# Attention, gating and experts given to the scheduler as one program instead of three stages

## The chip, the cores and the metric

The kernel runs on one core of a Trainium2 chip. The core has five instruction queues that run side by side and meet only at semaphores: TensorE (PE in the profile, its weight loads PEld), VectorE (DVE), ScalarE (ACT), GpSimd (POOL) and SyncE (SP, which here only starts DMAs). The metric is the device time of one execution in microseconds (us). Before the change it is 3069.19 us, the median of four runs that lie between 3068.82 and 3069.36 us.

## The reference: what is computed

Inputs are `q`, `k`, `v` of shape (8, 8, 576, 64) (batch B, heads H, sequence S, head dimension) and random features `omega` (128, 64). Attention is linear: each row of q and k becomes 128 positive features, and softmax is replaced by two small products per head.

```python
h  = x*scale @ omega.T - sum((x*scale)**2)/2
phi = exp(h - max(h)) / sqrt(128)
num = phi(q) @ (phi(k).T @ v)
den = phi(q) @ phi(k).sum(rows)
x   = num / (den + 1e-6)             # heads side by side: (8, 576, 512)
```

The result x goes into a mixture of E = 8 experts. Each token has 8 gate logits and a local gate. Where the local gate is below a half (and at the first token of a sequence) the token takes the expert with the largest logit, otherwise it keeps the expert of the token before it. The output is the softmax weight of that expert times `relu(x @ w1[e]) @ w2[e]`, with w1 of shape (512, 1024) and w2 of shape (1024, 512) for each expert. The kernel computes all 8 experts for every token and adds them up with weights that are zero for all but one.

## The kernel before, in words

The kernel is written in a framework that takes a program, records what reads and writes what, puts the instructions of each engine in an order of its own choice, and adds the semaphores. What limits its choice is the dependences and the tile pools: a tile in a pool of n buffers can be started only when the user of the buffer n tiles ago is done. Copies written as `nc.any` are given to ACT or DVE by the scheduler. Every engine then runs its list strictly in order, and an instruction that waits holds up all that stand behind it on that engine.

The work stands in three blocks, each in a `with` of its own pools, so that a block starts only when the pools of the one before it are given back (lines are those of the kernel before):

- **Attention** (lines 76 to 135). For each of 8 x 8 heads, five tiles of up to 128 rows (four of 128 and one of 64). A *k tile*: transpose k on PE (L87), copy (L89), project with omega (L91), row maximum on DVE (L93), exponential on ACT (L95), and accumulate the product with v into `kv_ps` (L99). A *q tile*: transpose (L108), copy (L110), project (L112), exponential (L119), transpose (L121), copy (L123), product with the head's kv (L125), reciprocal and scaling on DVE (L127, L129), transpose back (L131), copy (L133), and a store into `x_bridge`, a DRAM tensor of shape (512, tokens) (L134). All products of this block are float32. PSUM: five buffers for the tiles named `proj`, three for `kv_ps`.
- **Gating** (lines 138 to 203). For each batch b, five tiles: load x from DRAM, logits on PE (L154), softmax and expert choice in small DVE and ACT steps, two transposes (L181, L184); then a scan along the sequence in ten doubling steps on DVE (L189, L190), one reduction over partitions on POOL (L194). The weights are transposed to token rows (L200).
- **Experts** (lines 206 to 245). All weights lie in SBUF as bfloat16; their loads are issued on POOL at the very start of the kernel. For each of 9 groups `tg` of 512 tokens: load x (L223), and for each expert eight h groups (four matmuls over the 512 inputs into one bank, L231; ReLU on ACT into `hsb`, L234), each followed by four matmuls into four y banks (L236). After the eighth group DVE adds each of the four y banks, weighted, to `acc` (L240). Then `acc` is stored (L244). PSUM: two h banks and four y banks; SBUF: two x buffers and two `acc` buffers.

Of the kernel before, what the change touches and what calls it, by code (L numbers as in the profile page):

```python
# [18 lines left out]
def kernel(  # L19
# [12 lines left out]
    nc = tc.nc  # L32
# [7 lines left out]

# [12 lines left out]
    NTG = (T + TG - 1) // TG  # L53
    assert T % TG == 0

    x_dram = nc.dram_tensor("x_bridge", (D, T), F32, kind="Internal").ap()

# [4 lines left out]
    nc.vector.tensor_copy(ident_bf, ident)  # L62
    omegaT = consts.tile([Dh, M], F32)
# [11 lines left out]

    with tc.tile_pool(name="attn_sb", bufs=6) as sb, \
         tc.tile_pool(name="attn_sb2", bufs=4) as sb2, \
         tc.tile_pool(name="attn_ps", bufs=5, space=bass.MemoryType.PSUM) as ps, \
         tc.tile_pool(name="attn_ps2", bufs=3, space=bass.MemoryType.PSUM) as ps2:
        for b in range(B):  # L80
            for h in range(H):
                kv_ps = ps2.tile([M, Dh + 1], F32)
                for ti, (s0, nt) in enumerate(stile):
                    k_nat = sb.tile([128, Dh], F32, name="qk_nat")
                    nc.sync.dma_start(out=k_nat[:nt], in_=k[b, h, ds(s0, nt), :])
                    kT_ps = ps.tile([128, 128], F32, name="proj")
                    nc.tensor.transpose(kT_ps[:Dh, :nt], k_nat[:nt], ident[:nt, :nt])  # L87
                    kT = sb.tile([Dh, 128], F32, name="qkT")
                    nc.any.tensor_copy(kT[:, :nt], kT_ps[:Dh, :nt])  # L89
                    proj = ps.tile([128, M], F32, name="proj")  # L90
                    nc.tensor.matmul(proj[:nt], lhsT=kT[:, :nt], rhs=omegaTs, start=True, stop=True)  # L91
                    mxn = sb.tile([128, 1], F32, name="mxn")
                    nc.vector.reduce_max(mxn[:nt], proj[:nt], axis=AX, negate=True)  # L93
                    kp = sb.tile([128, M], F32, name="qkp")
                    nc.scalar.activation(kp[:nt], proj[:nt], Act.Exp, bias=mxn[:nt])  # L95
                    v_aug = sb.tile([128, Dh + 1], F32, name="v_aug")
                    nc.sync.dma_start(out=v_aug[:nt, :Dh], in_=v[b, h, ds(s0, nt), :])
                    nc.vector.memset(v_aug[:nt, Dh:Dh + 1], 1.0)
                    nc.tensor.matmul(kv_ps, lhsT=kp[:nt], rhs=v_aug[:nt],  # L99
                                     start=(ti == 0), stop=(ti == NST - 1))  # L100
                kv_sb = sb2.tile([M, Dh + 1], F32)
                nc.any.tensor_copy(kv_sb, kv_ps)

                for ti, (s0, nt) in enumerate(stile):
                    q_nat = sb.tile([128, Dh], F32, name="qk_nat")
                    nc.sync.dma_start(out=q_nat[:nt], in_=q[b, h, ds(s0, nt), :])
                    qT_ps = ps.tile([128, 128], F32, name="proj")
                    nc.tensor.transpose(qT_ps[:Dh, :nt], q_nat[:nt], ident[:nt, :nt])  # L108
                    qT = sb.tile([Dh, 128], F32, name="qkT")
                    nc.any.tensor_copy(qT[:, :nt], qT_ps[:Dh, :nt])  # L110
                    proj = ps.tile([128, M], F32, name="proj")
                    nc.tensor.matmul(proj[:nt], lhsT=qT[:, :nt], rhs=omegaTs, start=True, stop=True)  # L112
                    ksq = sb.tile([128, Dh], F32, name="qksq")
                    sq = sb.tile([128, 1], F32, name="sq")
# [161 lines left out]
```

## Time and profile before

| what | value |
|---|---|
| median of 4 runs | 3069.19 us |
| the profiled execution, its own time | 3069.36 us |
| its span in the trace | 3067.3 us |
| busy PE / PEld / DVE / ACT / POOL | 2372.0 / 1222.0 / 691.6 / 863.9 / 86.8 us |
| instructions | 28764 |
| mean granted TensorE clock | 0.999 |

The profile is one execution. Its page gives busy time of each engine, the span in 40 slices, and the chain of work that ended last. Other views of the same trace list groups of instructions by line (count, busy time, mean of one, idle time before them and who ended it), the single instructions in order of time, and the busy times in chosen stretches. A matmul's duration in the trace runs to the modelled end of its result, so that two matmuls that follow each other overlap; what a matmul costs PE is read from the distance of two starts.

### The profile page before, as it was taken

What the parts mean: (1) busy time and instruction counts of PE and PEld (TensorE: products, weight loads), DVE (VectorE), ACT (ScalarE), POOL (GpSimd) and SP (SyncE); (2) the same over time, 40 slices, a digit from 0 to 9 for tenths busy, and PEclk for the clock granted to TensorE, in tenths of its full rate; (3) what the DMA queues carried; (4) which work ended last, traced back from release to release, by engine and by line L of the source; (5) the groups of instructions that cost most, each with busy time, mean ns of one, the idle gap of its engine ahead of it and who ended that gap; (6) DMA issues with size and microseconds to landing.
All of it is one profiled execution on the core that took longest, in us unless ns stands there. A gap on an engine that the chain in (4) does not pass through costs nothing.

```text
span 3067.3 us, 28764 instructions
## 1 busy us (share of the span) xinstructions
PE 2372.0 (77%) x8792; PEld 1222.0 (40%) x8884; DVE 691.6 (23%) x2980; ACT 863.9 (28%) x2541; POOL 86.8 (3%) x147
## 2 busy tenths in 40 slices
PE   5666666666666666666666666669999999999999
PEld 3443433434434334344343344433333333333333
DVE  1121211211212112122121123751222221221212
ACT  2222222222222222222222222223333333333333
POOL 5100000000000000000000000110000000000000
PEclk9999999999999999999999999999999999999999
DMA  9400100001000001000010001210000000000000
GB/s 176 86 20 21 22 20 21 22 19 22 20 21 22 20 21 22 19 22 21 20 22 20 21 22 44 69 32 1 21 21 1 21 21 1 21 21 2 20 14 14
DMA packets 208298, 80.11 MB, mean 26 GB/s; under 512 B 153872, under 2 KB 199440, under 8 KB 208144
## 3 DMA queue, kind: packets, MB, share of 16 engines
q1 hardware_dynamic: 189136, 56.77, 8.2%
q0 software_dynamic: 19008, 21.50, 4.2%
q8 instruction: 70, 1.15, 0.2%
q14 instruction: 84, 0.69, 0.1%
HBM read 80.79 MB, written 18.87 MB: 32 GB/s over the span
## 4 chain that ended last, share of the span: by engine, by line
PE 74%; ACT 10%; DVE 9%; issue 5%; DMA 1%; SPq 0%; ACTq 0%; POOL 0%; DVEq 0%; POOLq 0%
PE y_ps L236 17%; PE h_ps L231 16%; PE proj L112 8%; PE proj L91 8%; PE proj L125 7%; PE proj L121 5%; PE proj L131 4%; ACT qkp L119 4%; PE kv_ps L99 3%; PE proj L87 3%; DVE oa L129 3%; ACT qpT L123 3%; DVE qkT L110 2%; DVE rden L127 2%; ACT oaT L133 2%
## 5 line engine op out<-in xcount | busy, mean ns | idle before, releaser
L236 PE MATMUL y_ps<-w_all,hsb 128*128 128x512 bf16 x2266 | 545.4, 381 | 3.9 <-ACT hsb L234 1.5
L231 PE MATMUL h_ps<-xT,w_all 128*128 128x512 bf16 x2250 | 541.0, 380 | 6.2 <-DMA xT<-x_bridge 3.5
L234 ACT ACTIVATE hsb<-h_ps 128x512 bf16<-128x512 f32 x576 | 343.8, 597 | 675.7 <-PE h_ps L231 671.6
L240 DVE SCALAR_TENSOR_TENSOR acc<-y_ps,w_all_t,acc 128x512 f32<-128x512 f32 x288 | 196.3, 745 | 771.9 <-PE y_ps L236 754.8
L231 PEld LDWEIGHTS <-w_all 128*128 128x128 bf16 x2304 | 225.6, 98 | 276.3 <-DMA xT<-x_bridge 2.9
L112 PE MATMUL proj<-omegaTs,qkT 64*128 64x128 f32 (+1 forms) x640 | 246.6, 487 | 110.9 <-DVE qkT L110 109.2
L236 PEld LDWEIGHTS <-hsb 128*128 128x128 bf16 x2304 | 179.5, 98 | 339.0 <-ACT hsb L234 199.7
L125 PE MATMUL proj<-kv_sb,qpT 128*128 128x65 f32 (+1 forms) x640 | 206.8, 425 | 110.1 <-ACT qpT L123 110.1
L91 PE MATMUL proj<-omegaTs,qkT 64*128 64x128 f32 (+1 forms) x640 | 247.0, 487 | 51.9 <-ACT qkT L89 48.4
L131 PE MATMUL proj<-ident,oa 128*64 128x128 f32 (+1 forms) x320 | 128.3, 401 | 186.3 <-DVE oa L129 185.1
L121 PE MATMUL proj<-ident,qkp 128*128 128x128 f32 (+1 forms) x320 | 145.6, 455 | 141.5 <-ACT qkp L119 133.0
L127 DVE RECIPROCAL rden<-proj 128x1 f32<-128x1 f32 (+1 forms) x320 | 53.3, 167 | 815.9 <-PE proj L125 815.9
L133 ACT COPY oaT<-proj 64x128 f32<-64x128 f32 (+1 forms) x320 | 79.5, 249 | 550.0 <-PE proj L131 550.0
L112 PEld LDWEIGHTS proj<-omegaTs,qkT 64*128 64x128 f32 (+1 forms) x640 | 145.7, 287 | 221.9 <-DVE qkT L110 208.2
L125 PEld LDWEIGHTS proj<-kv_sb,qpT 128*128 128x128 f32 (+1 forms) x640 | 146.3, 289 | 197.6 <-ACT qpT L123 197.6
L119 ACT ACTIVATE qkp<-proj,sq 128x128 f32<-128x128 f32 (+1 forms) x320 | 117.3, 366 | 350.0 <-PE proj L112 350.0
L91 PEld LDWEIGHTS proj<-omegaTs,qkT 64*128 64x128 f32 (+1 forms) x640 | 146.1, 288 | 121.2 <-ACT qkT L89 113.6
L99 PE MATMUL kv_ps<-v_aug,qkp 128*128 128x65 f32 (+1 forms) x640 | 179.6, 382 | 0.4 <-ACT qkp L95 0.3
L99 PEld LDWEIGHTS kv_ps<-v_aug,qkp 128*128 128x128 f32 (+1 forms) x640 | 172.0, 328 | 18.6 <-issue 17.4
L93 DVE TENSOR_REDUCE mxn<-proj 128x1 f32<-128x128 f32 (+1 forms) x320 | 92.8, 290 | 341.4 <-PE proj L91 341.3
L89 ACT COPY qkT<-proj 64x128 f32<-64x128 f32 (+1 forms) x320 | 79.5, 249 | 275.1 <-PE proj L87 266.0
L121 PEld LDWEIGHTS proj<-ident,qkp 128*128 128x128 f32 (+1 forms) x320 | 58.4, 182 | 235.3 <-ACT qkp L119 235.2
(59 smaller groups left out, 1359.7 us busy)
## 6 DMA issues: line engine op xcount, KB each, us to landing
out_dram<-acc SPq DMA_DIRECT2D x36, 256.0 KB, 4.9
w_all<-in_moe_w_dram POOLq DMA_DIRECT2D x32, 256.0 KB, 7.0
qk_nat<-in_k_dram SPq DMA_DIRECT2D x256, 32.0 KB, 1.7
v_aug<-in_v_dram SPq DMA_DIRECT2D x256, 32.0 KB, 1.9
w_all<-in_moe_w_dram POOLq DMA_DIRECT2D x64, 128.0 KB, 7.8
qk_nat<-in_q_dram SPq DMA_DIRECT2D x256, 32.0 KB, 1.7
x_bridge<-oaT SPq DMA_DIRECT2D x256, 32.0 KB, 1.8
xT<-x_bridge SPq DMA_DIRECT2D x128, 64.0 KB, 2.0
```

Of the source, the lines that this page charges most:

```text
L91: nc.tensor.matmul(proj[:nt], lhsT=kT[:, :nt], rhs=omegaTs, start=True, stop=True)
L99: nc.tensor.matmul(kv_ps, lhsT=kp[:nt], rhs=v_aug[:nt], start=(ti == 0), stop=(ti == NST - 1))
L112: nc.tensor.matmul(proj[:nt], lhsT=qT[:, :nt], rhs=omegaTs, start=True, stop=True)
L119: nc.scalar.activation(qp[:nt], proj[:nt], Act.Exp, bias=sq[:nt])
L121: nc.tensor.transpose(qpT_ps[:, :nt], qp[:nt], ident[:nt, :nt])
L125: nc.tensor.matmul(o_ps[:nt, :Dh + 1], lhsT=qpT[:, :nt], rhs=kv_sb, start=True, stop=True)
L131: nc.tensor.transpose(oaT_ps[:Dh, :nt], oa[:nt], ident[:nt, :nt])
L133: nc.any.tensor_copy(oaT[:, :nt], oaT_ps[:Dh, :nt])
L231: nc.tensor.matmul(h_ps, lhsT=w1_all[:, e, c, ts(fc, 128)], rhs=xT[:, c, :], start=(c == 0), stop=(c == DC - 1))
L234: nc.scalar.activation(hsb, h_ps, Act.Relu)
L236: nc.tensor.matmul(y_ps[st][:128, :], lhsT=hsb[:, ts(st, 128)], rhs=w2_all[:, e, fc, :], start=(fc == 0), stop=(fc == FC - 1))
L240: nc.vector.scalar_tensor_tensor(acc[:, st, :], in0=y_ps[st], scalar=w_all_t[:, tt, e:e + 1], in1=acc[:, st, :], op0=Alu.mult, op1=Alu.add)
```

## The change

Three things change, and the arithmetic of the attention and gating steps stays the same.

1. All pools are opened once, at the top, and stay open to the end. The eight PSUM banks are divided among the three parts for the whole time: four for attention (`tp`, each tile now a full bank), one for `kv`, one for gating (`lg`), one for h (`h_ps`), one for y (`y_ps`). SBUF buffers: 4 instead of 6 in attention, one x buffer and one `acc` for the experts instead of two. The parts become functions `attn(b)`, `gating(b)` and `moe(tg)`; the program text calls attention and gating batch by batch, then the nine expert groups. Nothing but dependences and buffers now keeps the scheduler from putting expert work among later attention work.
2. In the experts, `hsb` holds all eight h groups of an expert (two buffers), and the four y banks are filled one after another from one bank, eight matmuls each.
3. In batch 0 only, each of the seven float32 PSUM tiles of a k and q tile pair first gets a matmul of the identity with a block of zeros (`fill`), 128x512 bfloat16. It writes zeros that the real matmul then overwrites.

In the changed kernel the attention lines are L110 (transpose k), L116 (project k), L124 (kv), L134, L140, L151, L157, L165 (the five PE steps of a q tile), the fills L109, L115, L133, L139, L150, L156, L164; gating has L181, L205, L208, L225 on PE; the experts have L242 (h), L244 (ReLU), L248 (y), L251 (weighted add), L234 (load x), L236 (clear `acc`), L254 (store).

```diff
-    with tc.tile_pool(name="attn_sb", bufs=6) as sb, \
-         tc.tile_pool(name="attn_sb2", bufs=4) as sb2, \
-         tc.tile_pool(name="attn_ps", bufs=5, space=bass.MemoryType.PSUM) as ps, \
-         tc.tile_pool(name="attn_ps2", bufs=3, space=bass.MemoryType.PSUM) as ps2:
...
+    fill = consts.tile([128, 512], BF)
+    nc.vector.memset(fill, 0.0)
...
+    a_sb = ctx.enter_context(tc.tile_pool(name="a_sb", bufs=4))
+    a_sb2 = ctx.enter_context(tc.tile_pool(name="a_sb2", bufs=3))
+    a_ps = ctx.enter_context(tc.tile_pool(name="a_ps", bufs=4, space=bass.MemoryType.PSUM))
+    a_ps2 = ctx.enter_context(tc.tile_pool(name="a_ps2", bufs=1, space=bass.MemoryType.PSUM))
+    g_sb = ctx.enter_context(tc.tile_pool(name="g_sb", bufs=2))
+    g_pb = ctx.enter_context(tc.tile_pool(name="g_pb", bufs=1))
+    g_ps = ctx.enter_context(tc.tile_pool(name="g_ps", bufs=1, space=bass.MemoryType.PSUM))
+    m_x = ctx.enter_context(tc.tile_pool(name="m_x", bufs=1))
+    m_h = ctx.enter_context(tc.tile_pool(name="m_h", bufs=2))
+    m_o = ctx.enter_context(tc.tile_pool(name="m_o", bufs=1))
+    m_psy = ctx.enter_context(tc.tile_pool(name="m_psy", bufs=1, space=bass.MemoryType.PSUM))
+    m_psh = ctx.enter_context(tc.tile_pool(name="m_psh", bufs=1, space=bass.MemoryType.PSUM))
...
+                kT_ps = a_ps.tile([128, 512], F32, name="tp")
+                if b == 0:
+                    nc.tensor.matmul(kT_ps, lhsT=ident_bf, rhs=fill, start=True, stop=True)
+                nc.tensor.transpose(kT_ps[:Dh, :nt], k_nat[:nt], ident[:nt, :nt])
...
+    def moe(tg):
+        t0 = tg * TG
+        xT = m_x.tile([128, DC, TG], BF, name="mxT")
...
+        for e in range(E):
+            hsb = m_h.tile([128, FC, TG], BF, name="hsb")
+            for fc in range(FC):
+                h_ps = m_psh.tile([128, TG], F32, name="h_ps")
+                for c in range(DC):
+                    nc.tensor.matmul(h_ps, lhsT=w1_all[:, e, c, ts(fc, 128)],
+                                     rhs=xT[:, c, :], start=(c == 0), stop=(c == DC - 1))
+                nc.scalar.activation(hsb[:, fc, :], h_ps, Act.Relu)
+            for st in range(ST):
+                y_ps = m_psy.tile([128, D], F32, name="y_ps")
                 for fc in range(FC):
...
+                    nc.tensor.matmul(y_ps, lhsT=hsb[:, fc, ts(st, 128)],
+                                     rhs=w2_all[:, e, fc, :], start=(fc == 0), stop=(fc == FC - 1))
+                tt = tg * ST + st
+                nc.vector.scalar_tensor_tensor(acc[:, st, :], in0=y_ps, scalar=w_all_t[:, tt, e:e + 1],
+                                               in1=acc[:, st, :], op0=Alu.mult, op1=Alu.add)
...
+    for b in range(B):
+        attn(b)
+        gating(b)
...
+    for tg in range(NTG):
+        moe(tg)
```

Three places show how the instructions move. The names are the tiles; what stands in brackets is the semaphore that an instruction waits for.

The first is PE in the middle of the attention. Before, a 128-row q tile is five matmuls in a row, from one transpose of q to the next:

```order
L108 MATMUL proj<-ident,qk_nat 64x128 [waits DMAHW4_49]
L112 MATMUL proj<-omegaTs,qkT 128x128 [waits DVE_49]
L121 MATMUL proj<-ident,qkp 128x128 [waits Activation_49]
L125 MATMUL proj<-kv_sb,qpT 128x65 [waits Activation_49]
L131 MATMUL proj<-ident,oa 64x128 [waits DVE_49]
```

Now the same five steps have expert matmuls between them. In the tile shown, which belongs to the 27th of the 64 heads, there are 1, 3, 2 and 3 of them in the four gaps ("..." stands for the rest of a gap):

```order
L134 MATMUL tp<-ident,qk_nat 64x128 [waits DMAHW2_49]
L242 LDWEIGHTS w_all
L242 MATMUL h_ps<-mxT,w_all 128x512
L140 MATMUL tp<-omegaTs,qkT 128x128 [waits Activation_49]
L248 LDWEIGHTS hsb
L248 MATMUL y_ps<-w_all,hsb 128x512 [waits DVE_49]
...
L151 MATMUL tp<-ident,qkp 128x128 [waits Activation_49]
...
L157 MATMUL tp<-kv_sb,qpT 128x65 [waits Activation_49]
...
L165 MATMUL tp<-ident,oa 64x128 [waits DVE_49]
```

What moved: of the 4608 expert matmuls, 3250 stand ahead of the last attention matmul in PE's list (the first of them in batch 0's fifth head), and 1358 behind it. On average a gap of a 128-row q tile holds 2.2, 2.6, 1.7 and 3.2 of them, and the gap between L110 and L116 of a k tile holds 2.0.

The second place is PE in batch 0, where there is no expert work yet. The fills stand in the gaps, and the transpose and projection of the next q tile (L134, L140) now stand ahead of the transpose back of this one (L165):

```order
L157 MATMUL tp<-kv_sb,qpT 128x65 [waits Activation_49]
L134 MATMUL tp<-ident,qk_nat 64x128 [waits DMAHW5_49]
L139 LDWEIGHTS ident_bf
L139 MATMUL tp<-fill,ident_bf 128x512 [waits PE_49]
L140 MATMUL tp<-omegaTs,qkT 128x128 [waits Activation_49]
L165 MATMUL tp<-ident,oa 64x128 [waits DVE_49]
...
L151 MATMUL tp<-ident,qkp 128x128 [waits Activation_49]
```

What moved: in batch 0 a q tile no longer ends before the next one begins. In batches 1 to 7 the old order stands (L165, then L134). The fills are 280 in all.

The third is PE in the experts when the attention is over. Before, two h groups of four and two y groups of four alternate, and h has two banks (the numbers 18651 and 18662 are two tiles in two buffers):

```order
L231 MATMUL h_ps_18651<-xT_18574,w1_all_16124 128x512
...
L231 MATMUL h_ps_18662<-xT_18574,w1_all_16124 128x512
...
L236 MATMUL y_ps_18581<-w2_all_16125,hsb_18656 128x512
L236 MATMUL y_ps_18582<-w2_all_16125,hsb_18656 128x512
L236 MATMUL y_ps_18583<-w2_all_16125,hsb_18656 128x512
L236 MATMUL y_ps_18584<-w2_all_16125,hsb_18656 128x512
L236 MATMUL y_ps_18581<-w2_all_16125,hsb_18667 128x512
```

Now each h group waits for ACT and each y group for DVE, since the bank is the same one:

```order
L242 MATMUL h_ps_21949<-mxT_21573,w1_all_86 128x512 [waits Activation_49]
...
L248 MATMUL y_ps_21926<-w2_all_87,hsb_21847 128x512 [waits DVE_49]
...
L242 MATMUL h_ps_21955<-mxT_21573,w1_all_86 128x512 [waits Activation_49]
...
L248 MATMUL y_ps_21985<-w2_all_87,hsb_21936 128x512 [waits DVE_49]
...
L242 MATMUL h_ps_21961<-mxT_21573,w1_all_86 128x512 [waits Activation_49]
L242 MATMUL h_ps_21961<-mxT_21573,w1_all_86 128x512
...
L248 MATMUL y_ps_21985<-w2_all_87,hsb_21936 128x512
L242 MATMUL h_ps_21967<-mxT_21573,w1_all_86 128x512 [waits Activation_49]
```

What moved: for one expert the list is now h4 y8 h4 y8 h4 y8 h4 y3 h4 y1 h4 y1 h4 y1 h4 y1 y1 (a letter with the number of matmuls). Eight h groups each reuse one bank, four y groups each reuse one bank, and four of the h groups have only a single y matmul behind them.

291 lines of the change are left out of this document (136 added, 155 removed).

## Prediction

> **What bounds the kernel now.** I read the page first, for PE's share, its clock and the chain:
>
> ```profile
> PE   5666666666666666666666666669999999999999
> PEclk9999999999999999999999999999999999999999
> PE 74%; ACT 10%; DVE 9%; issue 5%; DMA 1%; SPq 0%; ACTq 0%; POOL 0%; DVEq 0%; POOLq 0%
> ```
>
> There are two regimes: PE busy at six tenths for two thirds of the span, then full. The clock is full in every slice. The busy times in three stretches give the stages (columns: stretch and length, then busy time and count of PE, PEld, DVE, ACT, POOL, then clock, DMA share, GB/s):
>
> ```profile
> 13.00:1880.00 1867.00, 1265.96 (x3832) 740.75 (x3832) 369.71 (x2167) 476.32 (x1724) 46.38 (x88) 1.00 0.15 30
> 1880.00:2043.00 163.00, 95.36 (x444) 76.11 (x444) 111.50 (x509) 42.51 (x240) 18.57 (x14) 1.00 0.25 60
> 2043.00:3067.30 1024.30, 1010.66 (x4516) 405.11 (x4608) 209.69 (x296) 343.82 (x576) 16.48 (x32) 1.00 0.06 14
> ```
>
> 13 us of start, attention to about 1880, gating to 2043, experts to the end. Only the experts fill PE; attention is a chain, as PE's instructions in order of time show (start, duration):
>
> ```profile
> 1009.18 0.42 PE L87 MATMUL proj<-ident,qk_nat 128*64 128x128 f32 x1
> ...
> 1012.22 0.42 PE L87 MATMUL proj<-ident,qk_nat 128*64 128x128 f32 x1
> 1012.43 0.53 PE L99 MATMUL kv_ps<-v_aug,qkp 128*128 128x65 f32 x2
> 1012.99 0.79 PE L91 MATMUL proj<-omegaTs,qkT 64*128 64x128 f32 x2
> 1013.71 0.42 PE L87 MATMUL proj<-ident,qk_nat 128*64 128x128 f32 x1
> ...
> 1016.55 0.42 PE L108 MATMUL proj<-ident,qk_nat 128*64 128x128 f32 x1
> ...
> 1020.89 0.42 PE L108 MATMUL proj<-ident,qk_nat 128*64 128x128 f32 x1
> 1021.75 0.79 PE L112 MATMUL proj<-omegaTs,qkT 64*128 64x128 f32 x2 [0.44 <-DVE qkT L110]
> 1023.06 0.48 PE L121 MATMUL proj<-ident,qkp 128*128 128x128 f32 x1 [0.52 <-ACT qkp L119]
> 1023.89 0.69 PE L125 MATMUL proj<-kv_sb,qpT 128*128 128x65 f32 x2 [0.35 <-ACT qpT L123]
> 1025.16 0.42 PE L131 MATMUL proj<-ident,oa 128*64 128x128 f32 x1 [0.58 <-DVE oa L129]
> 1025.38 0.42 PE L108 MATMUL proj<-ident,qk_nat 128*64 128x128 f32 x1
> ...
> 1038.34 0.42 PE L87 MATMUL proj<-ident,qk_nat 128*64 128x128 f32 x1
> ```
>
> A head takes 1038.34 - 1009.18 = 29.16 us, and 64 x 29.16 = 1866, which is the stage. Its five k tiles take 1016.55 - 1009.18 = 7.37; a 128-row q tile takes 1025.38 - 1020.89 = 4.49. In the q tile each step waits for ACT or DVE to bring back the last one's result. What a step occupies is less than its duration: a transpose lasts 0.42, but the next matmul starts 0.22 later (1025.16 to 1025.38). Taking that tail of 0.2 off, the five steps occupy 0.22 + 0.59 + 0.28 + 0.49 + 0.22 = 1.8 us, and PE is free for 0.64, 0.72, 0.55 and 0.78 us in the four gaps, 2.7 us in all.
>
> **What an expert matmul and its waits cost.** Rows of the expert stage, in order of time:
>
> ```profile
> 2167.13 1.89 PE L231 MATMUL h_ps<-xT,w_all 128*128 128x512 bf16 x8
> 2168.25 0.60 ACT L234 ACTIVATE hsb<-h_ps 128x512 bf16<-128x512 f32 x1 [2.05 <-PE h_ps L231]
> ...
> 2168.91 1.90 PE L236 MATMUL y_ps<-w_all,hsb 128*128 128x512 bf16 x7
> ...
> 2170.64 1.89 PE L231 MATMUL h_ps<-xT,w_all 128*128 128x512 bf16 x8
> ```
>
> Sixteen matmuls take 2170.64 - 2167.13 = 3.51 us, 0.219 each (one record of the y row is missing). 4608 of them are 1009 us, the stage. The first h group of four has entered PE by 2167.13 + 0.88 = 2168.01; its ReLU starts at 2168.25 and y, which reads it, at 2168.91. So **one use of an h bank costs 0.90 us** after the last matmul has entered. For a y bank:
>
> ```profile
> 2059.72 1.90 PE L236 MATMUL y_ps<-w_all,hsb 128*128 128x512 bf16 x8
> ...
> 2061.08 2.73 DVE L240 SCALAR_TENSOR_TENSOR acc<-y_ps,w_all_t,acc 128x512 f32<-128x512 f32 x4 [17.04 <-ACT hsb L234]
> ```
>
> ```profile
> L240 DVE SCALAR_TENSOR_TENSOR acc<-y_ps,w_all_t,acc 128x512 f32<-128x512 f32 x288 | 196.3, 745 | 771.9 <-PE y_ps L236 754.8
> ```
>
> The fifth matmul completes the first bank and has entered by 2059.72 + 5 x 0.219 = 2060.82; DVE starts 0.26 later and takes 0.745. With 0.05 for the semaphore (the gap from the ReLU's end at 2168.85 to y is 0.06) **one use of a y bank costs 1.06 us**. Before, other banks covered both.
>
> **The change part by part.**
>
> *Batch 0 (eight heads, no expert work).* The 280 fills are 280 x 0.219 = 61 us of PE. They stand in gaps: five per q tile are 1.1 us against 2.7 free. They gain nothing, since the clock is 1.00 already. What does gain is the new order, in which the next L134 and L140 go ahead of L165: the period is then L125's 0.49, then 0.86 (transpose to projection), 1.31 and 0.83 (the steps of the rows above), 3.49 us for 4.49. A k tile loses: L124 no longer fills the wait for the copy but stands with two fills ahead of L116: 0.21 + 0.56 + 0.44 + 0.59 = 1.8 us for 1.49. A head: five k tiles 9.0, first q tile 4.3, three at 3.5, the 64-row one 3.0: 26.8. I take **220 us for eight**; bounds 210, and 8 x 29.16 + 61 = 294 if nothing of it overlaps.
>
> *Batches 1 to 7 (56 heads, with 3250 expert matmuls, 58 a head).* The 9.7 expert matmuls of a q tile are 2.1 us against 2.7 free; gap by gap 0.48 of 0.64, 0.57 of 0.72, 0.37 of 0.55, 0.70 of 0.78. The chain therefore stays near 4.49. In a k tile two of them (0.44) hide in the wait between L110 and L116 (1012.22 to 1012.99, 0.77 between starts), but L124 now stands behind L116: 0.77 + 0.59 + 0.56 = 1.92 for 1.49. Five make 9.3 for 7.37. A head is then **31.1 us** if nothing collides. What is added per head:
>
> - ACT and DVE run in order. 7.3 ReLUs of 0.6 and 3.6 weighted adds of 0.745 make 7.1 us a head. They cost nothing where they fall while PE works, all 7.1 if each holds up a step of the chain. Most gaps leave ACT or DVE free for the better part of a microsecond, so I take 1.5, near the lower end. In it are the waits for the one h and y bank: between two uses there is mostly more than one attention step, over 1.06 us.
> - Gating now runs beside attention, and its 163 us as a stage go. Its PE and DVE work does not:
>
> ```profile
> L154 PE MATMUL lg<-wg,xT 128*128 128x9 f32 (+1 forms) x320 | 66.9, 336 | 40.0 <-ACT pe L165 17.0 <-issue 15.5 <-DMA xT<-x_bridge 4.0
> L181 PE MATMUL proj<-ident,sv 128*8 128x128 f32 (+1 forms) x40 | 14.4, 359 | 14.1 <-DVE sv L179 6.0 <-DVE rst L170 2.9 <-ACT seg_a L182 2.7
> L184 PE MATMUL proj<-ident,pe 128*8 128x128 f32 (+1 forms) x40 | 15.0, 375 | 3.6 <-ACT seg_a L182 2.4
> L189 DVE TENSOR_TENSOR seg_b<-seg_a 8x575 f32<-8x575 f32 (+4 forms) x40 | 26.8, 669 | 2.5 <-ACT seg_a L182 2.3
> ```
>
>   The PE rows are 96 us, 12 per batch; the scan's maxima, two such groups, about 6 per batch on DVE. Half of both on the path is 9 per batch, 1.1 a head (bounds 0 and 2.3). The SP queue also carries the loads of x and the stores of the result among the loads of q, k and v, which stand up to four buffers ahead; nothing is added.
> - One x buffer: a group's load starts when the last h of the group before is done.
>
> ```profile
> 2040.16 4.46 POOL L223 DMA_DIRECT2D xT<-x_bridge  x8 [2.15 <-DVE w_all L197]
> ...
> 2043.32 0.61 PE L231 MATMUL h_ps<-xT,w_all 128*128 128x512 bf16 x1 [2.24 <-DMA xT<-x_bridge]
> ...
> 2045.81 2.44 PE L231 MATMUL h_ps<-xT,w_all 128*128 128x512 bf16 x5 [1.02 <-DMA xT<-x_bridge]
> ```
>
>   The last part is there 5.65 us after the issue, and about 2.5 us of y work stands ahead: 3.2 a group, six groups, 0.35 a head. POOL's list has the weight loads first, as before, then x loads and gating's reductions, each of which stands where its input comes late anyway. The single `acc` waits for a store and a clear while eight h groups of the next expert run, and costs nothing unless DVE stands at the clear.
>
> The sum is 31.1 + 1.5 + 1.1 + 0.35 = 34.05, and **56 x 34.05 = 1907 us**. Bounds: 31.1 x 56 = 1742, and with 7.1, 2.3 and 0.6 in full 41.1 x 56 = 2302.
>
> *The rest of the experts (1358 matmuls, 21.2 experts).* In the pattern h4 y8 h4 y8 h4 y8 h4 y3 h4 y1 h4 y1 h4 y1 h4 y1 y1 each y group starts 0.88 after the last: short by 1.06 - 0.88 = 0.18, four times. An h group with y8 ahead waits for nothing; three with one y ahead are short by 0.90 - 0.22 = 0.68, and so is the last y1; one with three ahead by 0.06. In all 0.72 + 2.72 + 0.06 = 3.5 us on 64 x 0.219 = 14.0. 21.2 x 17.5 = 371; two x reloads and the last gating add about 12. **383 us**, where the kernel before would take 297.
>
> *End.* Before, the last add and store are
>
> ```profile
> 3061.30 2.73 DVE L240 SCALAR_TENSOR_TENSOR acc<-y_ps,w_all_t,acc 128x512 f32<-128x512 f32 x4 [11.33 <-PE y_ps L236]
> 3062.07 2.31 SPq L244 DMA_DIRECT2D out_dram<-acc  x4
> ```
>
> so the span ends 3.3 us after the last add; with 1.0 for the add, 4 to 5 us.
>
> Sum: 13 + 220 + 1907 + 383 + 5 = 2528 of span. The profiled execution's own time is 2.1 us above its span and 0.2 us from the median, so the time is **2530 us**, 17.6% below before. Put otherwise: 712 us of expert work and 163 of gating go under the attention, which grows by about 275 for it; the tail gives back 86.
>
> [...] The attention stretch has a gap of 0.35 to 0.58 us before four of five matmuls and still shows clock 1.00. [...]
>
> **The rivals.**
>
> - *ACT and DVE collide.* For it: 7.1 us a head of long instructions in in-order queues that also carry every chain step. Against it: ACT is busy 476 of 1867 us in attention. With two thirds of them on the path (4.8 for 1.5), the head is 37.3 and the time 2715; with all and the upper bounds 41.1 and 2925.
> - *Single banks in an in-order queue (slower).* If each h group and each y group in PE's list stands there until its bank is free, with the attention matmul behind it: 7.3 x 0.90 + 3.6 x 1.06 = 10.4 a head. With the 3.0 above, 31.1 + 10.4 + 3.0 = 44.5, 2492 for 56, and 3115 us. It is slower from (3067 - 621) / 56 = 43.7 a head on. Against it: mostly an attention step, which waits anyway, stands between two uses.
> - *The clock halves* in the tail: 64 x 0.219 more per expert, 21.2 x 14 = 297, 2825 us. The rows at 1.00 are against it.
> - *Less is lost*: collisions and gating wholly hidden, 31.1 to 32 a head, 2365 to 2415 us.
> - *The interleaving is not there*, because something holds the expert work back: then only the 163 of gating could go, and the tail's losses (72 x 3.5 = 252) make it slower; but PE's list fixes the order, and PE cannot leave it.
>
> **How the numbers follow.** Forecast, 32.3 to 38 a head, 2430 to 2750: 0.81. Collisions above that: 0.08. Less lost: 0.05. Slower: 0.04. Halved clock: 0.02. The range is 2430 to 2750. About 0.2% can be told from no change in this kernel; faster by more 0.95, within 0.01, slower 0.04.
>
> **What would show it.** Right: no separate gating stage; attention of batches 1 to 7 from about 235 to 2140 us, 34 us from one L110 of a head to the next; a q tile of 128 rows at 4.5 to 5; in the tail 17.5 us per expert with 0.6 to 0.7 idle before an L242 group, ended by ACT; clock 1.00. Wrong: idle before L242 or L248 ended by ACT or DVE while attention runs, of many tenths per group; chain steps that wait for a ReLU or an add; PE long idle for a DMA.

## The result, and the profile after

The median after is 2082.91 us, against 3069.18 before: a ratio of 0.6785 (95% interval 0.6775 to 0.6795). The forecast, 2530 in a range from 2430 to 2750, had the sign right and missed the size by 447 us; the time lies below the range. The one execution of the changed kernel that was first profiled was disturbed (4086 us, its bfloat16 matmuls some 0.62 us apart throughout), so the trace read here, called *after*, is of the same kernel run again: 2090.42 us, span 2088.7.

Its page: PE's busy row and its granted clock in 40 slices.

```profile
PE   6899999999999999999999999999999998888887
PEclk9898799999999999999988899999999999999999
```

Where PE was busy for six tenths of two thirds of the span, it is now full from the third slice until the rest of the experts begins. The stages: batch 0, batches 1 to 7 with expert work among them, and the rest of the experts (columns as before: stretch and length, busy time and count of PE, PEld, DVE, ACT, POOL, clock, DMA share, GB/s).

```profile
13.00:193.00 180.00, 163.81 (x763) 84.07 (x770) 46.96 (x279) 59.76 (x216) 48.01 (x91) 0.94 0.71 125
193.00:1704.00 1511.00, 1438.99 (x6866) 708.84 (x7000) 598.39 (x2680) 647.58 (x2015) 27.28 (x32) 0.97 0.16 35
1704.00:2088.70 384.70, 325.50 (x1366) 133.05 (x1393) 81.38 (x134) 103.99 (x187) 6.21 (x9) 0.99 0.05 12
```

Set against the terms of the sum: batch 0 took 180 us (220 forecast), the 56 heads 1511 (1907), the rest of the experts with the end 385 (388). Of the 439 us between the sum and this span, 396 lie in the 56 heads, 40 in batch 0 and 3 in the tail. One term failed, and the next view shows how. It is PE in order of time, in the middle of the interleaved part: a k tile from L110 to L110, then a q tile of 128 rows from L134 to L134.

```profile
1003.15 0.27 PE L110 MATMUL tp<-ident,qk_nat 128*64 128x128 f32 x1
1003.26 0.38 PE L242 MATMUL h_ps<-mxT,w_all 128*128 128x512 bf16 x1
...
1003.78 0.48 PE L116 MATMUL tp<-omegaTs,qkT 64*128 64x128 f32 x2
...
1004.57 0.24 PE L110 MATMUL tp<-ident,qk_nat 64*64 64x64 f32 x1
...
1005.79 0.27 PE L134 MATMUL tp<-ident,qk_nat 128*64 128x128 f32 x1
...
1009.30 0.30 PE L165 MATMUL tp<-ident,oa 128*64 128x128 f32 x1
1009.43 0.27 PE L134 MATMUL tp<-ident,qk_nat 128*64 128x128 f32 x1
```

The transposes, which do the same work as before, last 0.27 to 0.30 us for 0.42 and let the next matmul start after 0.11 (1003.15 to 1003.26); before it was 0.22. The projection lasts 0.48 for 0.79. So **the same float32 matmuls now run at about twice the rate**, though the clock row of before read 1.00 all through. The k tile takes 1.42 us here (1.32 in the median of the stretch), the q tile 3.64 (median 3.79), for 1.92 and 4.49 in the forecast, and with expert matmuls inside (two in this k tile, seven in this q tile).

The interleaved part can also be seen at half rate. From 197, 234, 1081 and 1142 us of this trace on, the clock row reads 0.50 for 20 to 24 us. The last of these stretches, and PE in it in order of time:

```profile
1142.20:1165.90 23.70, 22.27 (x64) 10.39 (x66) 5.63 (x29) 5.72 (x18) 0.00 (x0) 0.50 0.16 46
```

```profile
1150.60 0.42 PE L110 MATMUL tp<-ident,qk_nat 128*64 128x128 f32 x1
...
1151.13 1.06 PE L242 MATMUL h_ps<-mxT,w_all 128*128 128x512 bf16 x2
...
1152.84 0.42 PE L110 MATMUL tp<-ident,qk_nat 128*64 128x128 f32 x1
...
1158.02 0.42 PE L134 MATMUL tp<-ident,qk_nat 128*64 128x128 f32 x1
...
1163.42 0.42 PE L134 MATMUL tp<-ident,qk_nat 128*64 128x128 f32 x1
```

The k tile takes 2.24 us here, with two expert matmuls in it as above (2.33 in the median of 12 such tiles, 1.27 in that of the 208 at full rate). The q tile takes 5.40, with six for seven. At half rate throughout, the interleaved steps would have been longer than the forecast's 1.92 and 4.49, not shorter.

The moment of the change can be seen in batch 0 of the same trace:

```profile
21.07 0.42 PE L110 MATMUL tp<-ident,qk_nat 128*64 128x128 f32 x1
21.28 0.63 PE L115 MATMUL tp<-fill,ident_bf 128*128 128x512 bf16 x1
21.71 0.63 PE L109 MATMUL tp<-fill,ident_bf 128*128 128x512 bf16 x1
...
30.98 0.27 PE L151 MATMUL tp<-ident,qkp 128*128 128x128 f32 x1
31.09 0.38 PE L164 MATMUL tp<-fill,ident_bf 128*128 128x512 bf16 x1
31.30 0.38 PE L133 MATMUL tp<-fill,ident_bf 128*128 128x512 bf16 x1
```

At 21 us a transpose takes 0.21 and a fill 0.43; at 31 us it is 0.11 and 0.21.

The trace of before had held the sign all along, at the start of its expert stage. These are weight loads of one row of eight y matmuls, each of which waits for nothing but its turn:

```profile
2048.53 0.15 PEld L236 LDWEIGHTS <-hsb 128*128 128x128 bf16 x1 [0.28 <-issue]
2048.96 0.15 PEld L236 LDWEIGHTS <-hsb 128*128 128x128 bf16 x1 [0.28 <-issue]
...
2050.24 0.15 PEld L236 LDWEIGHTS <-hsb 128*128 128x128 bf16 x1 [0.28 <-issue]
2050.54 0.10 PEld L236 LDWEIGHTS <-hsb 128*128 128x128 bf16 x1 [0.15 <-issue]
```

They follow each other at 0.43 until 2050.24, where the rest of the stage has 0.219 for a matmul. PE came out of attention and gating at half rate and rose between 2050.24 and 2050.54 us, some 7 us after its first expert matmul (2043.32); a row that reads 1.00 there, and everywhere, can't be right, and neither can the mean granted clock of 0.999 in the table of before.

In the traces of before, of after, of the kernel of the change with fills of 32 columns and of that with two h and two y banks the row goes wrong in one place only: it reads 1.00 from the start until TensorE first rises to the full rate, although it runs at half rate until then. In before that is up to 2050 us, and all 1024 transposes of 128x128 in its attention last 0.39 us or more. From the first rise on the row agrees with the transposes in these traces. In after, 38 of them lie where it reads 0.50 and last 0.42 to 0.47, and the 978 where it reads 1.00 last 0.27 to 0.33.

### The profile page after: what moved, and what is told of

Same layout as the page of the kernel before. It is cut to its first block, busy times and chain, and to the rows that moved or that the text cites. A ratio compares the mean times of both kernels' runs of the same rounds, so it can differ in the third digit from the quotient of the medians.

```text
span 4084.4 us, 28391 instructions
## 1 busy us (share of the span) xinstructions
PE 3977.2 (97%) x8993; PEld 1500.6 (37%) x9164; DVE 741.5 (18%) x3104; ACT 831.8 (20%) x2418; POOL 86.8 (2%) x147
## 4 chain that ended last, share of the span: by engine, by line
PE 96%; ACT 2%; issue 2%; DVE 0%; SPq 0%; DMA 0%; ACTq 0%
PE h_ps L242 33%; PE y_ps L248 31%; PE tp L116 5%; PE tp L140 5%; PE kv L124 4%; PE tp L157 3%; PE tp L151 2%; PE tp L110 2%; PE tp L165 2%; PE tp L134 2%; ACT hsb L244 2%; PE lg L181 2%; PE tp L164 1%; PE tp L150 1%; PE tp L115 1%
## 5 line engine op out<-in xcount | busy, mean ns | idle before, releaser
L242 PE MATMUL h_ps<-mxT,w_all 128*128 128x512 bf16 x2228 | 1525.8, 802 | 35.6 <-issue 19.4
L248 PE MATMUL y_ps<-w_all,hsb 128*128 128x512 bf16 x2216 | 1534.7, 809 | 23.3 <-issue 15.9
L244 ACT ACTIVATE hsb<-h_ps 128x512 bf16<-128x512 f32 x576 | 344.0, 597 | 1191.2 <-PE h_ps L242 1159.6
L248 PEld LDWEIGHTS <-hsb 128*128 128x128 bf16 x2304 | 360.4, 163 | 522.9 <-issue 447.2
L242 PEld LDWEIGHTS <-w_all 128*128 128x128 bf16 x2304 | 328.1, 149 | 537.5 <-issue 491.6
L251 DVE SCALAR_TENSOR_TENSOR acc<-y_ps,w_all_t,acc 128x512 f32<-128x512 f32 x288 | 216.2, 751 | 1027.2 <-PE y_ps L248 976.4
L157 PEld LDWEIGHTS tp<-kv_sb,qpT 128*128 128x128 f32 (+1 forms) x640 | 185.3, 305 | 216.8 <-ACT qpT L153 127.8
L116 PE MATMUL tp<-omegaTs,qkT 64*128 64x128 f32 (+1 forms) x640 | 242.1, 507 | 7.9 <-issue 5.4
L140 PEld LDWEIGHTS tp<-omegaTs,qkT 64*128 64x128 f32 (+1 forms) x640 | 128.0, 241 | 322.6 <-ACT qkT L136 91.5
L116 PEld LDWEIGHTS tp<-omegaTs,qkT 64*128 64x128 f32 (+1 forms) x640 | 134.4, 253 | 301.5 <-ACT qkp L120 180.4
L140 PE MATMUL tp<-omegaTs,qkT 64*128 64x128 f32 (+1 forms) x640 | 234.3, 491 | 2.5 <-ACT qkT L136 1.4
L124 PEld LDWEIGHTS kv<-v_aug,qkp 128*128 128x128 f32 (+1 forms) x640 | 179.7, 326 | 84.7 <-issue 70.8
L124 PE MATMUL kv<-v_aug,qkp 128*128 128x65 f32 (+1 forms) x640 | 188.4, 388 | 1.2 <-ACT qkp L120 0.9
L157 PE MATMUL tp<-kv_sb,qpT 128*128 128x65 f32 (+1 forms) x640 | 172.3, 371 | 6.2 <-DVE qpT L153 4.5
L112 ACT COPY qkT<-tp 64x128 f32<-64x128 f32 (+1 forms) x300 | 74.5, 248 | 454.8 <-PE tp L110 453.1
L151 PE MATMUL tp<-ident,qkp 128*128 128x128 f32 (+1 forms) x320 | 154.8, 484 | 6.5 <-issue 5.3
L165 PE MATMUL tp<-ident,oa 128*64 128x128 f32 (+1 forms) x320 | 152.2, 476 | 1.8 <-issue 1.2
L134 PE MATMUL tp<-ident,qk_nat 128*64 128x128 f32 (+1 forms) x320 | 148.0, 462 | 0.0
```

What stands on the lines that cost most here:

```text
L116: nc.tensor.matmul(proj[:nt, :M], lhsT=kT[:, :nt], rhs=omegaTs, start=True, stop=True)
L124: nc.tensor.matmul(kv_ps, lhsT=kp[:nt], rhs=v_aug[:nt], start=(ti == 0), stop=(ti == NST - 1))
L140: nc.tensor.matmul(proj[:nt, :M], lhsT=qT[:, :nt], rhs=omegaTs, start=True, stop=True)
L151: nc.tensor.transpose(qpT_ps[:, :nt], qp[:nt], ident[:nt, :nt])
L157: nc.tensor.matmul(o_ps[:nt, :Dh + 1], lhsT=qpT[:, :nt], rhs=kv_sb, start=True, stop=True)
L165: nc.tensor.transpose(oaT_ps[:Dh, :nt], oa[:nt], ident[:nt, :nt])
```

## The experiments

Theory C: TensorE ran the attention of before at half rate, whatever the clock row says; work that leaves it little idle lifts the rate, and this is what the forecast lacked. Theory O: the rate is as the row says, and more work overlaps, or the new order of the steps is worth more, than was thought. In the kernels with fills the lines are shifted; the names of the tiles tell which step a row is (`qk_nat` in, a transpose of k or q; `omegaTs`, a projection; `oa`, the transpose back; `fill`, a fill).

**The same kernel again, and without the fills.** The first is the trace above. In the second no fill is issued:

```diff
-                if b == 0:
+                if b < 0:
                     nc.tensor.matmul(kT_ps, lhsT=ident_bf, rhs=fill, start=True, stop=True)
```

> The changed kernel once more, for its profile. Theory C (clock): in the kernel before, TensorE works in the attention stage at a lower rate than the granted clock of its profile (1.00) tells, and dense bfloat16 matmuls among the attention steps lift it. Then the granted clock of this profile is well below 1 in some early slices and 1 later, two transposes that follow each other start less than 0.15 us apart in batches 1 to 7 (0.22 before), and the distance from the transpose of q to its projection falls under 0.8 (0.86 before). Theory O (overlap alone): PE's steps keep the durations of the kernel before, and a head of batches 1 to 7 takes less than the 31.1 us of the prediction's lower bound because steps of neighbouring tiles overlap in PE's list.

> The changed kernel without the 280 zero matmuls of batch 0. Theory C: the expert matmuls lift the rate from batch 1 on as before, and only batch 0 falls back to about 29 us a head from 22 or so: 40 to 60 us slower than the changed kernel. If the lift needs the fills to begin, it is slower by several hundred. Theory O: the fills only cost, and it is 0 to 30 us faster.

Without fills 2136.83 us, ratio 0.6954 (0.6943 to 0.6966): the fills are worth 0.0169 of 3069, 52 us. Batch 0 ends at 255.6 for 192.5; its heads take 29 to 30 us, as in the kernel before, with transposes 0.21 to 0.22 apart. Batches 1 to 7 take 1501 us, as with fills (1511): there expert work does what the fills did (from 279 us on the transposes of 128x128 last 0.27 to 0.33, but for two stretches of about 20 us at half rate, from 720 and from 1200 us).

**Fills in the kernel before.** No interleaving at all, only the fills: in batch 0, and in all eight batches (2240).

```diff
-                    kT_ps = ps.tile([128, 128], F32, name="proj")
+                    kT_ps_f = ps.tile([128, 512], F32, name="proj")
+                    if b == 0:
+                        nc.tensor.matmul(kT_ps_f, lhsT=ident_bf, rhs=fill, start=True, stop=True)
+                    kT_ps = kT_ps_f[:, :128]
```

> The kernel before with the zero matmuls in batch 0 alone (280 of them; the tiles they fill are the same banks, widened). Theory C: batch 0's heads take 24 to 26 us instead of 29.16, the heads after it fall back to 29, and the whole is 25 to 45 us faster. Theory O: the fills cost up to 61 us, 3069 to 3130.

> The kernel before with the zero matmuls in all 8 batches (2240 of them, 491 us of PE at 0.219). Theory C: a head falls to 24 to 26 us throughout, the attention stage from 1867 to 1540 to 1660, and the whole to 2740 to 2870, though PE has more to do. Theory O: the fills lie in gaps at best, 3069 or more, up to 3500.

With fills in batch 0, one run, 3005.43 us, 64 us less than before, where Theory C expected 25 to 45. Its clock row, and a k tile of a late head:

```profile
PEclk8875555555555555555555555579999999999999
```

```profile
1003.49 0.42 PE L92 MATMUL proj<-ident,qk_nat 128*64 128x128 f32 x1
1004.26 0.79 PE L99 MATMUL proj<-omegaTs,qkT 64*128 64x128 f32 x2 [0.35 <-ACT qkT L94]
1004.98 0.42 PE L92 MATMUL proj<-ident,qk_nat 128*64 128x128 f32 x1
```

Here the row says a half, and the durations are those of before to the hundredth (0.42, 0.79, a k tile of 1.49). The same speed is put down as 1.00 in one trace (100 to 1860 us of before), which had not risen yet, and as 0.50 in the other (300 to 1800 us), which had. Its heads are 26.2, 26.9, 24.5 and 24.2 us, then 18.2 while the fills last, then some 29.1 again. The tiles of those late heads are widened too, without a fill, and PE's matmuls stand there in the order of before: so the widening by itself changes nothing. With fills in all batches 2388.52 us, ratio 0.7781 (0.777 to 0.7793): 2240 matmuls of zeros more, 681 us less, 18.2 us a head. It is at full rate from the fifth head on, which is Theory C's case, and faster than C's 24 to 26 us a head; but the fills also change the order of the steps, so the two had to be taken apart.

**The order without the work, and the work without the order.** Fills of 32 columns in all places and batches; and fills of 512 columns, two ahead of L112 and two ahead of L121 of before, which leave the order of the attention steps as it was.

```diff
+                    if True:
+                        nc.tensor.matmul(kT_ps_f[:, :32], lhsT=ident_bf, rhs=fill, start=True, stop=True)
```

```diff
+                    if True:
+                        nc.tensor.matmul(proj_f[:, :512], lhsT=ident_bf, rhs=fill, start=True, stop=True)
+                        nc.tensor.matmul(proj_f[:, :512], lhsT=ident_bf, rhs=fill, start=True, stop=True)
```

> The kernel before with 2240 fills of only 32 columns, one in each of the seven float32 tiles, in all batches. They give TensorE hardly any work, but they change the order in which the steps stand just as the wide fills do (the transpose and projection of the next q tile ahead of the transpose back of this one). Theory C (what the wide fills in all batches bring is the rate of TensorE): such small matmuls do not raise the rate, transposes stay 0.21 to 0.22 us apart, and the order alone gives 23 to 26 us a head, as in the first heads of the kernel with fills in batch 0: 2670 to 2870 us. Theory O (it is the new order, and the rate is the same): 18 to 19 us a head as with the wide fills, 2380 to 2440 us.

> The kernel before with two fills of 512 columns ahead of each q projection and two ahead of the transpose behind it, in all batches (1280 fills). The attention steps stand in the same order as before. Theory C: the fills raise the rate at least in the q tiles, transposes follow at 0.11 us, a q tile takes about 3.1 us for 4.49 and a head 20 to 23, 2500 to 2650 us. Theory O: with the old order nothing is gained, and the fills, longer than two of the gaps at the rate before, cost up to 2 us a head: 3070 to 3200 us.

The short fills give 2592.93 us, ratio 0.8446 (0.8433 to 0.8458), outside both expectations. Rows of a late head:

```profile
1008.89 0.40 PE L119 MATMUL proj<-ident,qk_nat 128*64 128x128 f32 x1
1009.09 0.23 PE L124 MATMUL proj<-fill,ident_bf 128*128 128x32 bf16 x1
```

The transpose takes 0.20: half rate, as C said. But a head takes 21.7 us for 29.16, so the order alone brings 477 us, more than C gave it. Theory O has this part, and falls with the other: 204 us of the 681 are still to come from the wide fills.

The 1280 long fills in the old order give 3357.89 us, ratio 1.0937 (1.092 to 1.0953), slower than both expected:

```profile
1008.21 0.42 PE L113 MATMUL proj<-ident,qk_nat 128*64 128x128 f32 x1
1008.42 0.63 PE L118 MATMUL proj<-fill,ident_bf 128*128 128x512 bf16 x1
1008.85 0.63 PE L119 MATMUL proj<-fill,ident_bf 128*128 128x512 bf16 x1
...
1011.98 0.69 PE L139 MATMUL proj<-kv_sb,qpT 128*128 128x65 f32 x2 [0.35 <-ACT qpT L136]
1013.25 0.42 PE L146 MATMUL proj<-ident,oa 128*64 128x128 f32 x1 [0.58 <-DVE oa L143]
```

The rate never rose: 0.21 for a transpose and 0.43 for a fill, although a quarter of the stage is such fills (1280 x 0.43 = 550 of some 2160 us). The gaps of 0.35 and 0.58 in each q tile are still there, and a head grows to 33.7 us. That bfloat16 work of itself lifts the rate is thereby wrong.

**How much work, and of which type.** Fills of 256 columns, and fills of 128 columns in float32, in all places and batches.

```diff
-    fill = consts.tile([128, 512], BF)
+    fill = consts.tile([128, 128], F32)
...
-                        nc.tensor.matmul(kT_ps_f, lhsT=ident_bf, rhs=fill, start=True, stop=True)
+                        nc.tensor.matmul(kT_ps_f[:, :128], lhsT=ident, rhs=fill, start=True, stop=True)
```

> The kernel before with fills of 256 columns in all seven tiles and all batches: the order of the kernel with fills of 32 columns (21.7 us a head, transposes 0.21 to 0.22 apart) and of that with 512 columns (18.2 us, 0.11 apart), with half the fill work of the latter. Theory D (the rate rises once fills of bfloat16 in this order leave TensorE little idle, whatever their length): transposes at 0.11, 35 fills of 0.11 a head, 15 to 18 us a head, 2160 to 2360 us. Theory H (half the fill work is too little for it): the rate stays, each fill takes 0.21, some of it beside other work, 22 to 27 us a head, 2600 to 2930 us.

> The kernel before with fills that are float32, 128 columns each (two passes, 0.6 us at the rate before by the projection's rows, against 0.43 for a bfloat16 fill of 512 columns), in all seven tiles and all batches. Theory B (the rate rises with TensorE's busy share, whatever the type): transposes at 0.11, 20 to 22 us a head, 2480 to 2610 us. Theory K (float32 work does not raise it; bfloat16 must be dense): transposes stay 0.21 to 0.22 apart, 35 fills a head add most of their 0.5 to 0.6 us, 33 to 42 us a head, 3300 to 3900 us.

256 columns: 2235.36 us, ratio 0.7273 (0.7254 to 0.7291), as D said. A head takes 15.5 us once the rate is up, which here took six heads (150 us). The float32 fills: 2453.92 us, ratio 0.8 (0.7985 to 0.8014), below the expectation of B by 26 us and far from that of K; 19.1 us a head. Rows of the two at 300 us:

```profile
300.48 0.30 PE L154 MATMUL proj<-ident,oa 128*64 128x128 f32 x1
300.61 0.27 PE L143 MATMUL proj<-fill,ident_bf 128*128 128x256 bf16 x1
300.72 0.27 PE L152 MATMUL proj<-fill,ident_bf 128*128 128x256 bf16 x1
```

```profile
301.05 0.27 PE L138 MATMUL proj<-ident,qkp 128*128 128x128 f32 x1
301.16 0.39 PE L117 MATMUL proj<-fill,ident 128*128 128x128 f32 x2
```

Full rate in both: fills in float32 lift the rate as fills in bfloat16 do. Stretches from within the attention stage, one row from each of five kernels: before, the long fills in the old order, 32 columns, 256 columns, float32 (the first numbers are the stretch, its length and PE's busy time):

```profile
100.00:1860.00 1760.00, 1194.76 (x3622) 699.06 (x3622) 349.47 (x2050) 449.78 (x1629) 0.00 (x0) 1.00 0.10 21
```

```profile
100.00:2170.00 2070.00, 1737.17 (x4911) 861.66 (x4910) 357.60 (x2137) 445.76 (x1595) 0.00 (x0) 1.00 0.08 18
```

```profile
100.00:1390.00 1290.00, 1226.66 (x5653) 820.86 (x5652) 363.16 (x2165) 397.53 (x1459) 1.30 (x3) 1.00 0.13 29
```

```profile
160.00:1030.00 870.00, 850.52 (x5313) 524.77 (x5311) 295.36 (x1845) 429.99 (x1565) 0.00 (x0) 1.00 0.18 39
```

```profile
150.00:1240.00 1090.00, 1089.53 (x7419) 900.19 (x7419) 311.35 (x1823) 454.29 (x1655) 0.00 (x0) 1.00 0.15 32
```

Busy 68%, 84% and 95%: half rate. Busy 98% and 100%: full rate. All five rows give the clock as 1.00, the first three because no rise had come yet. Between 32 and 256 columns the head falls from 21.7 to 15.5 us, 358 us in the whole time, although its 35 fills are longer. Part of this may be order: 886 of the 7444 other matmuls stand in another place, all of them in the attention.

The kernel with 256 columns parts the two by itself. Its fifth and its seventh head have the same matmuls on PE in the same order:

```profile
102.60:126.90 24.30, 24.30 (x96) 15.03 (x95) 5.28 (x33) 7.83 (x29) 0.53 (x1) 0.50 0.34 62
149.60:165.10 15.50, 15.15 (x96) 9.34 (x95) 5.28 (x33) 7.65 (x29) 0.00 (x0) 1.00 0.18 39
```

One takes 24.3 us at half rate, the other 15.5 at full rate: on PE nothing but the rate differs. The first row also shows that the busy share does not set the rate by itself, as PE is busy for all of those 24.3 us at half rate; and in the tail of after it holds the full rate at 85% (325.50 of 384.70 us, clock 0.99). What the hardware counts stays open: the busy share contains the modelled ends of matmuls, and no run varied it in small steps.

**The fills of the change, cut to 32 columns.** This splits the 52 us of the fills in batch 0.

```diff
-                    nc.tensor.matmul(kT_ps, lhsT=ident_bf, rhs=fill, start=True, stop=True)
+                    nc.tensor.matmul(kT_ps[:, :32], lhsT=ident_bf, rhs=fill[:, :32], start=True, stop=True)
```

> The kernel after with the 280 fills of batch 0 cut from 512 to 32 columns: the new order of the steps in batch 0 stays, nearly all the work of the fills goes. Theory D (short fills leave TensorE too idle for the higher rate, the order alone gives 21.7 us a head as in the kernel before with fills of 32 columns): transposes in batch 0 stay 0.21 to 0.22 apart, its eight heads take 22 to 25 us, some 20 us more than after in batch 0, between after and the kernel without fills: 2095 to 2120 us. Rival (all that the fills bring in batch 0 is their order): no later than after, 2065 to 2090 us.

2089.72 us, ratio 0.6824 (0.6803 to 0.6845), just below the range of D and just inside that of the rival. The trace sides with D: transposes in batch 0 are 0.20 apart, its heads 21.5 to 26.9 us. But the batch ends at 198.5 against 192.5, so of the 63 us by which batch 0 ends earlier with wide fills than with none (255.6), 57 are the order and 6 the rate, where D had 20. With the wide fills the rate goes up and down in the first three heads (full from 29 us, half again from 53, 63 and 84 us for 3 to 14 us each), which take 26.4, 29.8 and 25.2 us; the fills pay back in the five later ones, 19 to 21.

**Banks.** Two banks for h, for y, or for both, taken from attention's four.

```diff
-    a_ps = ctx.enter_context(tc.tile_pool(name="a_ps", bufs=4, space=bass.MemoryType.PSUM))
+    a_ps = ctx.enter_context(tc.tile_pool(name="a_ps", bufs=3, space=bass.MemoryType.PSUM))
-    m_psh = ctx.enter_context(tc.tile_pool(name="m_psh", bufs=1, space=bass.MemoryType.PSUM))
+    m_psh = ctx.enter_context(tc.tile_pool(name="m_psh", bufs=2, space=bass.MemoryType.PSUM))
```

> The kernel after with two h banks and three banks for attention, for one and four. 3618 expert matmuls then stand ahead of the last attention matmul for 3250, and 988 behind it for 1358. Theory S (the single h bank costs the tail what the prediction said, 2.7 us an expert, and the interleaved part is bound by TensorE): 368 matmuls more at 0.219 inside add 81 us there, the tail falls from 385 to about 240: 2010 to 2040 us. Rival A (attention needs its four banks): the tail falls the same, but each of the 56 heads waits for banks by 1.5 us or more beyond that, 2090 to 2150 us.

> The kernel after with two y banks and three banks for attention, for one and four. 3605 expert matmuls stand ahead of the last attention matmul and 1003 behind it. Theory S: 355 matmuls more inside add 78 us, the tail keeps most of its waits for the h bank (15.7 experts at 16.5 to 17, 265 us): 2035 to 2065 us, behind the kernel with two h banks. Rival A (attention needs its four banks): 2090 to 2170 us.

> The kernel after with two h and two y banks and two banks for attention in place of four. 3611 expert matmuls stand ahead of the last attention matmul, 997 behind it, as with two h banks alone. Theory S (attention is covered by expert work and needs no more banks; two h banks already take most of the tail's waits): within 20 us of the kernel with two h banks, 1975 to 2015 us. Rival A (attention's steps wait for a bank once there are only two): the heads grow by 1 us or more, 2050 to 2250 us.

Two h banks: **1994.58 us, ratio 0.649 (0.6462 to 0.6517)**, faster than both kernels. Two y banks: 2058.55 (0.6704, 0.6684 to 0.6724). Both: 2049.85 (0.6658, 0.6619 to 0.6696). The tail of after, then that with two h banks, in order of time:

```profile
1896.46 0.38 PE L248 MATMUL y_ps<-w_all,hsb 128*128 128x512 bf16 x1
1897.31 1.02 PE L242 MATMUL h_ps<-mxT,w_all 128*128 128x512 bf16 x4 [0.47 <-ACT hsb L244]
1898.17 0.38 PE L248 MATMUL y_ps<-w_all,hsb 128*128 128x512 bf16 x1
...
1903.67 1.89 PE L248 MATMUL y_ps<-w_all,hsb 128*128 128x512 bf16 x8 [0.19 <-DVE acc L251]
...
1906.40 1.89 PE L248 MATMUL y_ps<-w_all,hsb 128*128 128x512 bf16 x8
```

```profile
1910.32 1.89 PE L248 MATMUL y_ps<-w_all,hsb 128*128 128x512 bf16 x8
1912.05 1.24 PE L242 MATMUL h_ps<-mxT,w_all 128*128 128x512 bf16 x5
1913.13 1.89 PE L248 MATMUL y_ps<-w_all,hsb 128*128 128x512 bf16 x8
```

The waits for ACT are gone, and the tail is 232 us (1755.5 to 1987.8) for 385. Theory S had the tail right and the rest too dear: 368 matmuls more in the 56 heads lengthen them from 1511 to 1536 us, 24 us where 81 were expected (by one trace of each). So the 56 heads are not bound by TensorE's work alone; most of what is put there is still hidden. Three banks cost 27 us in batch 0 (it ends at 219.8). The kernel with two y banks came in as Theory S expected. Both together missed S's 1975 to 2015 us and lie just under Rival A's 2050. With two banks for attention the tail stays at 228 us and the 56 heads at 1547, and the loss lies in batch 0, which ends at 266.4: Rival A holds there, where little expert work covers a wait for a bank, and hardly elsewhere (the median of the later heads is 25.7 us, for 25.1 with three banks).

## Why the prediction was wrong

- **The step that failed** is the reading of the first view, "The clock is full in every slice", and what was built on it: that the fills "gain nothing, since the clock is 1.00 already", and that a k or q tile keeps the step times of before when expert work is put among them. The rows of before give step times at half rate; the expert matmuls were priced at full rate, 0.219. The sum mixed the two. With the steps of the rows above, 1.32 for 1.92 us a k tile and 3.64 to 3.79 for 4.49 a q tile, a head takes 25.1 us (the median distance of its first L110 from that of the next head) for the 31.1 of the sum: 6.0 x 56 = 336 of the 396 us. That this difference is the rate is shown by the stretches at half rate in the same trace, with 2.24 us for a k tile and 5.40 for a q tile of the same steps.
- **The surcharges** (collisions 1.5, gating 1.1, x reload 0.35: 2.95 a head) came to 27.0 - 25.1 = 1.9, and not all of it is what they stood for. The first heads of a batch, with gating beside them, take 29 to 42 us; but heads of 35.6, 32.3 and 35.3 us that start no batch lie on the stretches at half rate from 234, 1081 and 1142 us, for which the sum had no term.
- **Batch 0**: 180 for 220 (which was 8 x 26.8 = 214 and 6 us that the prediction does not account for). Here the size of the order was off as much as the rate. With fills of 32 columns, all at half rate, it took 188, and a q tile 2.73 us (two L134 at 146.12 and 148.85) where the sum had 3.49 for the new order; the k tiles were about right (9.1 for five in the median of the eight heads, 9.0 forecast).
- **The tail**: 385 for 388, with the pattern of h and y groups as worked out. The single steps were 0.63 short (0.85 from one-y group to the next h, less 0.22) for 0.68, and (2.73 - 12 x 0.219) = 0.10 for 0.18.
- **Waits for the single banks** while attention runs stayed small, as the forecast had it and against the slower rival. The group of h matmuls between 250 and 1600 us of after:

```profile
L242 PE MATMUL h_ps<-mxT,w_all 128*128 128x512 bf16 x1406 | 446.6, 385 | 32.4 <-ACT hsb L244 18.1 <-DMA mxT<-x_bridge 4.6 <-issue 2.4
```

  18 us of waiting for a ReLU in some 50 heads, 0.4 a head, and 2 us for the y bank, where the rival put 7.3 x 0.90 = 6.6 on the h bank.
- **The rivals** held one with the right direction, "less is lost", but from the same half-rate steps, so its 2365 was out of reach of 2083 as well. The clock was a rival too, in the wrong direction: that it might fall. That it was low already, and could rise, was left out.
- **Gaps and the full rate.** That the tail would keep the full rate with 0.68 idle after an h group rested on the row at 1.00 in before's attention, beside gaps of 0.35 to 0.58 us. That row is no evidence, as no rise had come yet. In the tail of after the full rate held all the same: with 0.47 idle ahead of an h group, its four matmuls still enter in 0.86 us (1897.31 to 1898.17). But the rate also fell without gaps of that length: in after it fell at 197 us, when the fills had ended (the last starts at 192.31), and from 183 us to there no idle time of PE was longer than 0.14 us. What length or number of gaps matters is not shown.

## What to carry to other kernels

Check the clock row against the spacing of a known matmul (here a float32 transpose, 0.21 or 0.11 us to the next start, and a 512-column bfloat16 matmul, 0.43 or 0.22) in each stage before any duration of one stage is added to those of another. A 1.00 that stands ahead of the first lower value of the row is no evidence by itself (before's attention stood at 1.00 with its transposes at 0.21). Where TensorE waits often and briefly, work that fills the gaps can be worth more than the time it hides, since it can raise the rate of all the rest (wide fills in all batches took a head of before from 29.16 to 18.2 us, short ones to 21.7); half-measures cost (the long fills in the old order made the kernel 9% slower). And price an order of steps by itself: it brought 477 us with no work worth the name behind it.

## What the runs showed of the hardware

- TensorE's rate over a stretch of the attention stage was a half at 68% busy (before), 84% (the long fills in the old order) and 95% (32 columns), and full at 98% (256 columns, bfloat16) and 100% (float32 fills). But it was a half at 100% busy in the fifth head with fills of 256 columns (24.30 of 24.30 us), and full at 85% in the tail of after (325.50 of 384.70 us), so the busy share does not set it by itself. The first rise came at 29 us in after; with fills of 256 columns the rate was still a half from 102.60 to 126.90 us and full from 149.60 to 165.10.
- The granted clock of a trace read 1.00 up to the first rise even where TensorE ran at half rate (100 to 1860 us of before, with transposes 0.39 us long and more; 100 to 1390 us of the kernel with fills of 32 columns, with 0.40; 100 to 2170 us of that with the long fills in the old order, with 0.42). Behind the first rise of after it agreed with the length of the transposes.
- Transposes of 128x128 followed the rate: in after, behind the first rise, 0.42 to 0.47 us long at a clock of 0.50 and 0.27 to 0.33 at 1.00.
